# Routed attention and a gated FFN on one core: preparation placed by a table, one more pair turned on TensorE, v summed by adds, a last tile in parts

## The chip, the core and the metric

The kernel runs on one core of one Trainium2 chip. The time is the device time of the whole program in microseconds; for the kernel before it is the median of 3 runs. One further execution was profiled. Its instructions are named by engine: PE (TensorE), PEld (its weight loads), DVE (VectorE), ACT (ScalarE), POOL (GpSimd) and SP (SyncE, which here only issues DMAs).

## The reference

Attention in which a query sees only the keys of its own cluster, followed by a gated FFN. Shapes: q, k, v 4 x 8 x 768 x 64 (batch, heads, rows, width), 16 centroids a head, FFN 512 to 1536 to 512, all float32.

```python
q_assign = argmax(q_n @ c_n.T); k_assign = argmax(k_n @ c_n.T)     # rows normalised
mask = q_assign[..., :, None] == k_assign[..., None, :]
scores = where(mask, (q @ k.T) / 8, -1e9)
attn = softmax(scores)                                              # + 1e-9 in the sum
x = (attn @ v).transpose(0, 2, 1, 3).reshape(3072, 512)
out = (sigmoid(x @ w_gate) * (x @ w_val)) @ w_out
```

## The kernel before, in words

**Steps.** The eight heads of a batch are taken in four pairs. One *step* is 128 keys against 384 queries of one head: a score matmul on PE (`do_scores`, L434), an exponential on ACT (L439), and, two steps later, three matmuls with v (`do_av`, L451). A head has 12 steps, a batch 96, the program 384; the step number runs through all batches. In every batch the last pair (heads 6 and 7) is taken in two halves of queries, so its four runs have six steps each, and head 7 is first used at step 78 of the batch.

**Mask.** Nothing compares clusters. Each head has a tile T of 80 rows: 64 of turned k and q and 16 of one-hot planes, for k the one-hot and for q minus 1920 wherever the cluster is another one. The score matmul over 80 rows thus adds the mask. To build T: the float32 data is split into a high and a low half in fp16 (tile hl: a cast, then a subtraction), turned, matmul'd with the centroids (logits lg), the maximum is picked (tile oh), the one-hots are turned and evicted into rows 64 to 79.

**Two ways to do that.** `pieces` (batch 0) turns on PE: tu (PE transposes, L545), ev (eviction, L556 on DVE or L554 on ACT), lg (L248), pk (a maximum and two comparisons on DVE), ot (one-hots turned on PE, L582), pl0 and pl1 (their evictions, L592 and L596, or L594 on ACT); hi and lo are the split (L527, L534). `pair_prep` (batches 1 to 3) turns by DMA from SP's queue: sp (the split, L679 and L680), turn (a DMA transpose of hl into T), lgt (logits, L257, with a copy of their low half on ACT, L263), pk (five DVE instructions, L271 to L284), ot (a DMA transpose of the one-hots, L693) and hops (four small DMAs into T, L305).

**Sums of v.** Where a key is masked its exponential is 0, so a small multiple of the sum of all v is added before the division. In batch 0 PE sums (`v_sum_pe`, L200). In the others one DVE instruction reduces 6 rows of v a partition (`v_sum`, L182, strided), one matmul with ones adds the partitions (L188), and DVE scales (L193). When a head ends, DVE adds that sum to the result and takes reciprocals (`normalise`, L216 and L218), and POOL multiplies (L221); x is then turned by DMA, or for the last pair of batch 0 on PE (L470, evicted at L471).

**Order.** Every engine works through its instructions in the order in which the program issues them; the order is written by hand. `at(i, f)` puts f behind step i. The due times stand as offsets to the step in which a head is used: `OFF` for `pieces`, numbers in `pair_prep` for the others, constant for all heads. `OFF` counts 12 steps a head for head 7 too. The loads of the next inputs are issued 76 steps ahead, the weights one block every ten steps from step 8.

**FFN.** A batch's rows are computed in two halves of 384. `ffn_atoms` makes a list of small functions: 12 gate atoms (four matmuls into one PSUM bank, L319, a tanh on ACT, L325), 12 value atoms (L334, evicted with the product into hT on DVE, L339), and for each of three output tiles three atoms of four matmuls (L351), an eviction on ACT (L360) or DVE (L358) and a store (L361). `run_steps` puts the first half into a queue at step 92 of its batch and the second at step 8 of the next; `ffn_run` takes atoms out in every step, as long as a credit of 500 ns a step lasts (a gate or value atom is priced at 643 ns, an output atom at 864). What is left behind step 383 runs at the end. So PE has no FFN work in the first 92 steps.

**Buffers.** Scores, gates, values and logits share four PSUM banks (`ring`); output tiles and the turns on PE share two (`op`); av has two. Raw inputs have four buffers a kind.

**Lead-in.** Seven matmuls on a tile of zeros (`dummies`, L514) run while the first data is loaded; then the centroids are normalised and head 0 is prepared in two parts, and ACT loads the table for Exp (L158) before it evicts.

Of the kernel before, what the change touches and what calls it, by code (L numbers as in the profile page):

```python
# [16 lines left out]
def kernel(
# [152 lines left out]
    VA, SV = {}, {}  # L170

# [6 lines left out]
    def v_sum(b, p):  # L178
        s = svp.tile([128, 2, 65], HP, tag="vs", name="vs")
        POOL.memset(s[:, :, 64:65], float(NCH))  # L180
        with nc.allow_low_precision("sums of the fp16 values' sources"):
            DVE.tensor_reduce(  # L182
                s[:, :, 0:64], RAW["v", b, p].rearrange("p h c d -> p h d c"), AX.X, ALU.add
            )

        def rest():
            t = bank(130, name="vs_ps")
            PE.matmul(  # L188
                out=t, lhsT=ones, rhs=s.rearrange("p h d -> p (h d)"), start=True, stop=True
# [120 lines left out]
    def ffn_atoms(xT, t0, n, b, ch):  # L310
# [131 lines left out]
    def do_av(s):  # L442
# [13 lines left out]
        if last:  # L456
            normalise(av, nq, b, p, e, x[:, :, bass.ts(e, 64)])
            if e == 1:
                f = lambda: turn_x(b, p, x, 384 * s["h0"], nq, s["xT"])
                if b == 0 and p == NP - 1:  # L460
                    at(step_no[0] + 5, f)
                else:
                    f()

    def turn_x(b, p, x, o, nq, xT):
        dst = xT[:, p, o : o + 128 * nq].rearrange("p (c t) -> p c t", t=128)
        if b == 0 and p == NP - 1:
            ps = bank(NCH * 128, HP, name="x_ps")
# [11 lines left out]

    def run_bg(i):
# [3 lines left out]
    LA = 2  # L485
# [3 lines left out]
    def run_steps(heads, xT, second, first):  # L489

        done = 0
        for n, th in heads:
            for s in th():
                s["xT"] = xT
                do_scores(s)
                pend.append(s)
                if second and done == LAG:
                    second()
                if done == 84 + LAG:
                    first()  # L500
                ffn_run(FFN_NS)
                if len(pend) > LA:
                    do_av(pend.pop(0))
                run_bg(step_no[0])
                step_no[0] += 1
                done += 1

    LAG = 8
    FFN_NS = 500.0

    def dummies(n):
        for i in range(n):
            w = bank(512, name="wm")
            PE.matmul(out=w, lhsT=warm[:, 0:128], rhs=warm, start=True, stop=True)  # L514

    def pieces(p, e, parts=1):
# [7 lines left out]
        def hi(s, eng=None):  # L524
            if s == 0:
                st["hl"] = hlp.tile([128, 12, 128], HP, tag="hl", name="hl")
            (eng or DVE.tensor_copy)(  # L527
                st["hl"][:, 6 * s : 6 * s + 6, 0:64], RAW["kq"[s], 0, p][:, e]
            )

        def lo(s, eng=None, part=None):
# [3 lines left out]
                hl[:, :, 64:128], RAW["kq"[s], 0, p][:, e, a - 6 * s : z - 6 * s],  # L535
# [39 lines left out]
        def ot(part=0):  # L575
            n = NCH // parts
            st["oh", part] = []
            for r0_, m in ((64 * e, 64),) if parts == 1 else ((0, 32), (32, 32)):
                ps = turns(128 * n, name="oh_ps")
                st["oh", part].append(ps)  # L580
                for c in range(n):
                    PE.transpose(  # L582
                        ps[r0_ : r0_ + m, bass.ts(c, 128)],
                        ohx[p][:, n * part + c, r0_ : r0_ + m], identh,
                    )
# [33 lines left out]
    oh_zero(2)  # L619
    a["tu"](0, 0)  # L620
# [5 lines left out]
    a["ev"](1, None, 0)  # L626
# [142 lines left out]
```

## Time and profile before

| | us |
|---|---|
| median of 3 runs (lowest, highest) | 351.84 (350.81, 353.98) |
| the profiled execution's own time | 351.25 |
| its span, first to last instruction | 349.5 |
| busy in the span: PE, ACT, DVE, POOL | 331.3, 231.6, 181.4, 109.4 |
| first score matmul starts | 9.56 |
| end of the span behind the last PE matmul (345.44) | 4.0 |

In rows of the timeline the columns are: start, length, engine, line, operation, written tile <- read tiles, shape, count, and in brackets the idle time just before it with what ended it. Rows of groups give the busy time, the mean in ns and the idle time before them. A busy PE is a PE with a matmul in flight; consecutive matmuls overlap.

### The profile page before, as it was taken

Reading aid. Unit: us, or ns where it says so; the run is one execution under the profiler, and the core shown is the slowest. Engines: PE = TensorE matmul, PEld = TensorE weight load, DVE = VectorE, ACT = ScalarE, POOL = GpSimd, SP = SyncE. Lnnn points to the kernel's source line nnn. Section 1 sums busy time; section 2 is a strip of 40 time slices with the busy share of each in tenths; the row PEclk is TensorE's granted clock in tenths of the full one; section 3 lists DMA queues with packets and bytes.
Section 4 is the critical chain, followed back from the end, with each engine's and each line's share of the span. In section 5 each row is a group of like instructions: output and inputs, shape, how many; then the busy total and the mean of one; then the engine's idle time right before and its main releaser. Section 6 shows DMA issues by size and latency. Waiting matters only on the chain.

```text
span 349.5 us, 8661 instructions
## 1 busy us (share of the span) xinstructions
PE 331.3 (95%) x3272; PEld 204.6 (59%) x3272; DVE 181.4 (52%) x465; ACT 231.6 (66%) x531; POOL 109.4 (31%) x170
## 2 busy tenths in 40 slices
PE   7899987898999999999999999999999999999995
PEld 3766664565556655565656655566556655654652
DVE  4677876666536463657446563656354432441430
ACT  6478766776768876787768866787768766531330
POOL 5376966442313334333314233333301001100000
PEclk9699989899999999999999999999999999999999
DMA  7968999999357735767468536951542002101002
GB/s 231 375 122 125 205 240 203 201 215 255 76 115 218 129 135 126 201 147 185 92 118 233 134 103 144 226 104 33 122 119 48 10 3 86 52 0 62 30 0 90
DMA packets 83385, 46.40 MB, mean 133 GB/s; under 512 B 61584, under 2 KB 80272, under 8 KB 83344
## 3 DMA queue, kind: packets, MB, share of 16 engines
q1 hardware_dynamic: 77408, 41.11, 47.3%
q0 software_dynamic: 5792, 4.72, 9.6%
q8 instruction: 25, 0.41, 0.5%
q14 instruction: 16, 0.13, 0.1%
q10 hardware_dynamic: 144, 0.03, 0.0%
HBM read 28.34 MB, written 6.29 MB: 99 GB/s over the span
## 4 chain that ended last, share of the span: by engine, by line
PE 76%; DVE 9%; DMA 7%; issue 3%; ACT 2%; POOL 1%; POOLq 0%; ACTq 0%; DVEq 0%
PE o L351 17%; PE v L334 17%; PE g L319 15%; PE sc L434 13%; PE av L451 9%; DMA T<-hl 6%; PE lg L257 2%; DVE hT L339 2%; DVE vs L182 2%; ACT es L439 2%; PE t_ps L545 1%; DVE t L216 1%; DVE hl L679 1%; POOL hl L534 1%; PE lg L248 1%
## 5 line engine op out<-in xcount | busy, mean ns | idle before, releaser
L439 ACT ACTIVATE es<-sc 128x384 f16<-128x384 f32 x384 | 173.7, 492 | 60.7 <-PE sc L434 41.0
L434 PE MATMUL sc<-T 80*128 80x384 f16 x384 | 120.7, 334 | 2.5 <-DVE T L596 1.3
L451 PEld LDWEIGHTS <-es 128*128 128x128 f16 x1152 | 81.5, 99 | 57.1 <-ACT es L439 13.6
L451 PE MATMUL av<-va,es 128*128 128x65 f16 x1152 | 99.7, 196 | 2.5 <-DVE hl L679 0.6
L339 DVE SCALAR_TENSOR_TENSOR hT<-th,v 128x384 f16<-128x384 f32 x96 | 53.1, 553 | 76.6 <-PE av L451 46.2
L319 PE MATMUL g<-xTb,wg 128*128 128x384 f16 x384 | 78.6, 325 | 1.6 <-DVE xTb L471 0.4
L334 PE MATMUL v<-xTb,wv 128*128 128x384 f16 x384 | 78.1, 325 | 1.4 <-DVE hT L339 1.4
L351 PE MATMUL o<-wo,hT 128*128 128x512 f16 x288 | 71.3, 378 | 0.0
L325 ACT ACTIVATE th<-g 128x384 f32<-128x384 f32 x96 | 47.2, 492 | 28.6 <-DVE hT L339 16.3
L221 POOL TENSOR_TENSOR xp<-t,rec 128x384 f16<-128x384 f32 (+1 forms) x40 | 28.1, 702 | 118.5 <-DVE rec L218 54.7
L334 PEld LDWEIGHTS <-wv 128*128 128x128 f16 x384 | 37.2, 97 | 23.3 <-issue 3.5
L319 PEld LDWEIGHTS <-wg 128*128 128x128 f16 x384 | 37.2, 97 | 22.5 <-issue 2.2
L351 PEld LDWEIGHTS <-hT 128*128 128x128 f16 x288 | 28.0, 97 | 24.9
L434 PEld LDWEIGHTS <-T 80*128 80x128 f16 x384 | 37.6, 98 | 1.4 <-DVE T L592 0.5
L680 POOL TENSOR_TENSOR hl<-kraw,hl 128x384 f16<-128x384 f32 x24 | 21.9, 914 | 49.7 <-issue 38.8
L216 DVE TENSOR_TENSOR t<-av,sv 128x390 f32<-128x390 f32 (+1 forms) x40 | 19.1, 478 | 22.1 <-PE av L451 22.1
L680 POOL TENSOR_TENSOR hl<-qraw,hl 128x384 f16<-128x384 f32 x24 | 21.9, 912 | 11.0 <-DVE hl L679 10.9
L358 DVE TENSOR_SCALAR ob<-o 128x512 f32<-128x512 f32 x8 | 5.5, 692 | 33.1 <-PE o L351 33.1
L360 ACT ACTIVATE ob<-o 128x512 f32<-128x512 f32 x16 | 9.6, 597 | 17.1 <-PE o L351 17.0
L182 DVE TENSOR_REDUCE vs<-vraw 128x128 f16<-128x768 f32 x12 | 17.5, 1460 | 0.0
L257 PE MATMUL lg<-cm,T 128*128 128x32 f16 x288 | 11.0, 177 | 2.3 <-DMA T<-hl 2.3
L176 POOL CAST va<-vraw 128x768 f16<-128x768 f32 x15 | 13.1, 872 | 0.0
(70 smaller groups left out, 201.5 us busy)
## 6 DMA issues: line engine op xcount, KB each, us to landing
vraw<-in_v_dram SPq DMA_DIRECT2D x16, 384.0 KB, 5.1
out_dram<-ob SPq DMA_DIRECT2D x24, 256.0 KB, 2.2
kraw<-in_k_dram SPq DMA_DIRECT2D x15, 384.0 KB, 4.2
qraw<-in_q_dram SPq DMA_DIRECT2D x15, 384.0 KB, 4.5
wg<-in_moe_w_gate_dram POOLq DMA_DIRECT2D x4, 384.0 KB, 5.7
wv<-in_moe_w_val_dram POOLq DMA_DIRECT2D x4, 384.0 KB, 6.3
wo<-in_moe_w_out_dram POOLq DMA_DIRECT2D x2, 768.0 KB, 9.2
T<-ohT SPq DMA_DIRECT2D x48, 24.0 KB, 1.9
```

Source lines behind the costliest of these rows:

```text
L182: DVE.tensor_reduce(s[:, :, 0:64], RAW["v", b, p].rearrange("p h c d -> p h d c"), AX.X, ALU.add)
L216: DVE.tensor_tensor(t[:, 0:nq, :], av, sv, ALU.add)
L221: (eng or POOL).tensor_tensor(x, t[:, 0:nq, 0:64], bcast(rec[:, 0:nq], 64), ALU.mult)
L319: PE.matmul(out=g[:, 0:n], lhsT=wg[fc // WQ][:, dc, fc % WQ, :], rhs=xT[:, dc, t0 : t0 + n], start=(dc == 0), stop=(dc == NDC - 1),)
L325: ACT.activation(th[:, 0:n], g[:, 0:n], AF.Tanh, scale=0.5)
L334: PE.matmul(out=w[:, 0:n], lhsT=wv[fc // WQ][:, dc, fc % WQ, :], rhs=xT[:, dc, t0 : t0 + n], start=(dc == 0), stop=(dc == NDC - 1),)
L339: DVE.scalar_tensor_tensor(hT[:, fc, 0:n], st[0][:, 0:n], 1.0, w[:, 0:n], ALU.add, ALU.mult)
L351: PE.matmul(out=o, lhsT=hT[:, fc, bass.ts(t, 128)], rhs=wo[fc // 6][:, fc % 6, :], start=(fc == 0), stop=(fc == NFC - 1),)
L434: PE.matmul(out=sc.rearrange("p (c t) -> p c t", t=128), lhsT=s["k"], rhs=s["q"], start=True, stop=True,)
L439: ACT.activation(es, sc, AF.Exp, scale=SCALE)
L451: PE.matmul(out=av[:, s["c0"] + i, :], lhsT=s["es"][:, bass.ts(i, 128)], rhs=VA[b, p][:, e, s["j"], :], start=(first and i == 0), stop=(la ...
L680: POOL.tensor_tensor(hl[:, :, 64:128], r, hl[:, :, 0:64], ALU.subtract)
```

## The change

Every step number of the preparation, of the loads of weights and inputs, of the FFN's entries and its credit a step is now looked up in a table, `SCHED`. `h2ev1` is piece ev1 of head 2 in batch 0, `g0`, `g1` are heads 0 and 1 of batch 1; their numbers are steps of the program. `b1p2lg0` is a piece of pair 2 in batch 1, `b2...` of any pair in batches 2 and 3; their numbers are relative to the pair's first step. A name with E at its end puts a piece on another engine (A is ACT, D is DVE, P is POOL). `w..` and `wo.` are weights, `vc`, `vs`, `vu`, `vt` the parts of v's cast and sum, `lag` and `ns` the FFN's entry and credit, `dm` counts of spare matmuls.

- Batch 1's first pair is prepared by `pieces` and turned on PE (`npe: 1`), no longer by DMA.
- The first use of heads 6 and 7 is counted as it is (steps 72 and 78).
- The lead-in has 12 spare matmuls of 512 columns instead of 7, and 2, 6, 11 and 2 of 128 columns at four later places. ACT makes one more of the first evictions, loads the Exp table later, and gives a plane to DVE and the cast of v to POOL.
- `v_sum` adds with three DVE instructions in two pieces instead of one reduce.
- The last output tile of all is computed in column parts of 256, 128 and 128, each with its own eviction and store.

```diff
+SCHED = {
+    "halved0": 1, "npe": 1, "npe0": 4, "vs00": 5, "h1tu0": 0, "h1ev0": 0, "h1tu1": 0,
+    "h1ev1": 1, "h1lg": 2, "h1pk": 3, "h1ot": 6, "h1pl0": 10, "h1pl1": 11, "h2hi0": 0,
+    "h2lo0": 0, "h2hi1": 0, "h2lo1": 1, "h2tu0": 2, "h2ev0": 3, "h2tu1": 3, "h2ev1": 10,
+    "h2lg": 10, "h2pk": 12, "h2ot": 13, "h2pl0": 15, "h2pl1": 20, "h3hi0": 0, "h3lo0": 4,
+    "h3hi1": 1, "h3lo1": 4, "h3tu0": 11, "h3ev0": 12, "h3tu1": 15, "h3ev1": 16, "h3lg": 18,
+    "h3pk": 19, "h3ot": 20, "h3pl0": 24, "h3pl1": 30, "vc01": 13, "vs01": 24, "h4hi0": 4,
...
+    "h6lg": 63, "h6pk": 65, "h6ot": 67, "h6pl0": 69, "h6pl1": 69, "h7hi0": 22, "h7lo0": 40,
+    "h7hi1": 45, "h7lo1": 53, "h7tu0": 60, "h7ev0": 62, "h7tu1": 58, "h7ev1": 64, "h7lg": 65,
+    "h7pk": 65, "h7ot": 69, "h7pl0": 75, "h7pl1": 72, "vc03": 47, "vs03": 69, "g0hi0": 57,
+    "g0lo0": 66, "g0hi1": 67, "g0lo1": 70, "g0tu0": 77, "g0ev0": 78, "g0tu1": 81, "g0ev1": 81,
+    "g0lg": 81, "g0pk": 81, "g0ot": 87, "g0pl0": 87, "g0pl1": 92, "g1hi0": 69, "g1lo0": 78,
+    "g1hi1": 77, "g1lo1": 78, "g1tu0": 85, "g1ev0": 86, "g1tu1": 87, "g1ev1": 90, "g1lg": 93,
+    "g1pk": 93, "g1ot": 100, "g1pl0": 100, "g1pl1": 106, "w00": 3, "w01": 13, "w10": 26,
+    "w11": 20, "w20": 15, "w21": 35, "w30": 39, "w31": 65, "wo0": 73, "wo1": 91, "b1p0vc": -18,
+    "b1p0vs": -11, "b1p0vu": -2, "b1p0vt": 5, "b1p0ld": -80, "b1p1sp00": -59, "b1p1sp01": -53,
+    "b1p1tn0": -50, "b1p1lg0": -35, "b1p1pk0": -31, "b1p1sp10": -48, "b1p1sp11": -43,
+    "b1p1tn1": -40, "b1p1lg1": -24, "b1p1pk1": -24, "b1p1ot": -22, "b1p1hp0": -21,
...
+    "b1p2sp00": -58, "b1p2sp01": -54, "b1p2tn0": -54, "b1p2lg0": -32, "b1p2pk0": -29,
...
+    "b1p3vc": -15, "b1p3vs": -14, "b1p3vu": -5, "b1p3vt": 4, "b1p3ld": -79, "b2sp00": -59,
+    "b2sp01": -50, "b2tn0": -48, "b2lg0": -37, "b2pk0": -36, "b2sp10": -52, "b2sp11": -44,
+    "b2tn1": -40, "b2lg1": -27, "b2pk1": -27, "b2ot": -19, "b2hp0": -11, "b2hp1": -17,
+    "b2vc": -17, "b2vs": -15, "b2vu": -13, "b2vt": 4, "b2ld": -83, "xt30": 2, "xt31": 5,
+    "lag00": 8, "lag01": 7, "lag10": 6, "lag11": 10, "ns0": 530, "ns1": 470, "ns2": 500,
+    "ns3": 440, "dm0": 12, "dm1": 2, "dm2": 6, "dm3": 11, "dm4": 2, "la0": 2, "la1": 2,
+    "lgop": 0, "h2pl1E": "A", "h2lo0E": "D", "h4hi0E": "P", "h1ev0E": "A", "h3hi0E": "A",
+    "h4pl1E": "A", "g0hi1E": "A", "h5lo1E": "D", "h5ev0E": "A", "h6hi0E": "A", "g0ev1E": "A",
+    "h7hi1E": "P", "h4hi1E": "P", "h4lo0E": "D", "g1hi0E": "A", "h7hi0E": "A", "h3pl1E": "A",
+    "h4lo1E": "D", "h5lo0E": "D", "g1lo0E": "D", "h5hi1E": "A", "h3ev0E": "A", "h3hi1E": "A",
+    "h5hi0E": "P", "g0hi0E": "P",
+}
...
     def v_sum(b, p):
...
+        r, st = RAW["v", b, p], {}
+        def one():
+            st["a"] = vsp.tile([128, 2, 3, 64], FP, tag="va3", name="va3")
+            DVE.tensor_tensor(st["a"], r[:, :, 0:3], r[:, :, 3:6], ALU.add)
+        def two():
+            a = st["a"]
+            s = st["s"] = vss[(b * NP + p) % len(vss)]
+            t = vsp.tile([128, 2, 64], FP, tag="va1", name="va1")
+            DVE.tensor_tensor(t, a[:, :, 0], a[:, :, 1], ALU.add)
+            DVE.tensor_tensor(s[:, :, 0:64], t, a[:, :, 2], ALU.add)
...
+        def closing(t, a, z):
+            def f():
+                w = z - a
+                o = bank(w, name="o_end")
+                for fc in range(NFC):
+                    PE.matmul(
+                        out=o, lhsT=hT[:, fc, bass.ts(t, 128)],
+                        rhs=wo[fc // 6][:, fc % 6, a:z],
+                        start=(fc == 0), stop=(fc == NFC - 1),
+                    )
...
-    dummies(7)
+    dummies(SCHED.get("dm0", 7))
...
-    a["ev"](1, None, 0)
+    a["ev"](1, ACT, 0)
     centroid_d(cv)
     a["ev"](0, ACT, 1)
     a["ev"](1, ACT, 1)
-    v_cast(0, 0, ACT.copy)
+    ACT.activation(r1, warm[:, 0:1], AF.Exp)
     a["lg"](0)
     b_["hi"](0)
     b_["lo"](0)
+    v_cast(0, 0)
     a["lg"](1)
     a["pk"](0)
+    dummies(SCHED.get("dm2", 6), 128)
     a["ot"](0)
+    dummies(SCHED.get("dm3", 8), 128)
     a["pl"](0, None, 0)
-    a["pl"](1, ACT, 0)
+    a["pl"](1, None, 0)
...
+            lag = SCHED.get(f"lag{key}{i}", 8)
+            if b == B - 1 and i:
+                break
+            at(u + lag, lambda xT=xT, b=b, i=i: ffn_block(xT, 384 * i, 384, b, CH[i]))
...
+                ffn_run(SCHED.get(f"ns{b}", 500.0))
```

More of the change, by code (lines that the diff above doesn't have):

```diff
@@ L57 @@
     svp = pool("sv", 6)
+    vsp = pool("vs", 1)
     ohp = pool("oh", 2)
@@ L193, in rest @@
             DVE.tensor_scalar(sv.rearrange("p h d -> p (h d)"), t, TINY, None, ALU.mult)
-        return rest
+        return one, two, rest
     def v_sum_pe(b, p):
-        t = bank(130, name="vs_ps")
+        t = (turns if SCHED.get("lgop", 1) else bank)(130, FP, name="vs_ps")
         for j in range(NCH):
@@ L483, in run_bg, with dummies, pieces @@
             f()
-    LA = 2
+    LA = {0: SCHED.get("la0", 3), 1: SCHED.get("la1", 2)}
     pend = []
[L489 to L511, printed above, removed]
+    def dummies(n, m=512):
+        if not n:
+            return
+        w = bank(512, name="wm")
         for i in range(n):
-            w = bank(512, name="wm")
-            PE.matmul(out=w, lhsT=warm[:, 0:128], rhs=warm, start=True, stop=True)
-    def pieces(p, e, parts=1):
+            PE.matmul(out=w[:, 0:m], lhsT=warm[:, 0:128], rhs=warm[:, 0:m], start=True, stop=True)
+    def pieces(b, p, e, parts=1):
         h, st = 2 * p + e, {}
@@ L619 @@
     oh_zero(2)
+    for t in vss:
+        POOL.memset(t[:, :, 64:65], float(NCH))
+    dummies(SCHED.get("dm1", 3), 128)
     a["tu"](0, 0)
@@ L642, with halved, heads @@
     oh_zero(0)
+    def halved(b):
+        return SCHED.get("halved0", 1) if b == 0 else 1
+    def heads(b):
+        n = NP - halved(b)
+        out = [(p, e, [0, 1]) for p in range(n) for e in range(2)]
+        return out + [(p, e, [c]) for c in range(2) for p in range(n, NP) for e in range(2)]
+    USE, u = {}, 0
+    for p, e, c in heads(0):
+        USE.setdefault((p, e), u)
+        u += NCH * len(c)
+    at(0, lambda: dummies(SCHED.get("dm4", 2), 128))
     at(0, lambda: a["ot"](1))
@@ new lines @@
+    plan("vs00", 5, lambda: v_sum_pe(0, 0))
+    for b, p, e in P:
+        if b + p + e == 0:
+            continue
+        d = P[b, p, e]
+        u = USE[p, e] if b == 0 else 96 + 24 * p + 12 * e
+        for k_, o_ in OFF.items():
+            if b + p == 0:
+                if k_ not in first_b:
+                    continue
+                o_ = first_b[k_] - u
+            f = d[k_[:2]]
+            nm = f"{'hg'[b]}{2 * p + e}{k_}"
+            if k_[2:]:
+                eng = SCHED.get(nm + "E")
+                s_ = int(k_[2])
+                if k_[:2] == "hi":
+                    eng = eng and {"P": POOL.tensor_copy, "A": ACT.copy}[eng]
+                elif eng:
+                    eng = {"D": DVE, "A": ACT}[eng]
+                f = (lambda f=f, s_=s_, eng=eng: f(s_, eng)) if k_[:2] != "tu" else (
+                    lambda f=f, s_=s_: f(s_))
+            plan(nm, u + o_, f)
@@ L733 @@
+        for p, e, c in heads(b):
+            for s in head_steps(b, p, e, c):
+                s["xT"] = xT
+                do_scores(s)
+                pend.append(s)
+                ffn_run(SCHED.get(f"ns{b}", 500.0))
+                while len(pend) > LA[min(b, 1)]:
+                    do_av(pend.pop(0))
+                run_bg(step_no[0])
+                step_no[0] += 1
     while pend:
-        ffn_run(FFN_NS)
+        ffn_run(500.0)
         do_av(pend.pop(0))
+    assert not bg, sorted(bg)
```

151 lines of the change are left out of this document (78 added, 73 removed), and 11 rows, old and new, of the table SCHED.

## The prediction

> **What bounds the kernel now.** First the pace: each of the 384 steps issues one score matmul (tile sc), so the busy time by stretch, kept to that tile, counts steps. Columns: stretch, its length, PE busy (count), ACT busy (count), granted clock, DMA share, GB/s.
>
> ```profile
> 9.56:19.64 10.08, 4.72 (x13) 4.78 (x11) 0.66 1.01 357
> 19.64:44.73 25.09, 13.88 (x47) 19.89 (x48) 1.00 0.89 143
> 44.73:68.65 23.92, 12.22 (x36) 15.34 (x36) 0.86 1.08 205
> 71.37:148.98 77.61, 29.67 (x96) 44.16 (x97) 1.00 0.71 162
> 148.98:226.03 77.05, 29.65 (x97) 44.22 (x97) 1.00 0.65 151
> 226.03:300.90 74.87, 29.54 (x96) 43.74 (x97) 1.00 0.29 69
> ```
>
> The stretches are steps 0-11, 12-56, 57-92 (to the score of step 93), then batches 1, 2 and 3; counts hold what an edge cuts. Batch 0, which has no FFN beside it, has three paces: 0.84 us a step (10.08 / 12), 0.56 (25.09 / 45) and 0.66 (23.92 / 36). From step 93 on the FFN fills PE: 0.81, 0.80, and 0.78 in the last batch, beside which nothing is prepared. The same view for all engines (PE, PEld, DVE, ACT, POOL, clock, DMA):
>
> ```profile
> 6.54:9.96 3.42, 1.96 (x40) 1.29 (x37) 2.50 (x11) 2.29 (x6) 1.06 (x2) 1.00 1.02 342
> 9.96:16.78 6.82, 6.76 (x78) 5.40 (x75) 4.03 (x12) 2.90 (x6) 2.96 (x4) 0.50 1.07 379
> 19.64:44.73 25.09, 23.45 (x368) 16.19 (x367) 18.96 (x50) 19.89 (x48) 18.75 (x25) 1.00 0.89 143
> 57.75:61.16 3.41, 1.97 (x24) 1.11 (x25) 1.97 (x5) 2.12 (x6) 3.39 (x6) 1.00 1.08 210
> 61.16:64.57 3.41, 3.41 (x40) 2.49 (x39) 2.42 (x8) 3.35 (x9) 0.90 (x3) 0.50 0.78 115
> ```
>
> Twice a stretch with PE busy under 60% is followed by one at half clock. From 9.96 to 16.78 PE is full at half clock: the slow first steps are PE's. Next PE's own rows in order of time, in which two waits of batch 0 and 1 stand out: a mask plane evicted one step before its use, and a transpose by DMA that lands late.
>
> ```profile
> 59.30 0.32 PE L434 MATMUL sc<-T 80*128 80x384 f16 x1 [1.31 <-DVE T L596]
> ```
>
> ```profile
> 80.59 0.47 PE L257 MATMUL lg<-cm,T 128*128 128x32 f16 x12 [0.85 <-DMA T<-hl]
> ```
>
> Last, the FFN stretch: what DVE does, and PE beside it.
>
> ```profile
> 83.36 0.56 DVE L216 TENSOR_TENSOR t<-av,sv 128x390 f32<-128x390 f32 x1
> 83.95 0.19 DVE L218 RECIPROCAL rec<-t 128x6 f32<-128x6 f32 x1
> 84.06 1.46 DVE L182 TENSOR_REDUCE vs<-vraw 128x128 f16<-128x768 f32 x1
> 85.43 0.35 DVE L679 CAST hl<-kraw 128x384 f16<-128x384 f32 x1
> 85.70 0.55 DVE L339 SCALAR_TENSOR_TENSOR hT<-th,v 128x384 f16<-128x384 f32 x1
> ```
>
> ```profile
> 81.81 0.33 PE L434 MATMUL sc<-T 80*128 80x384 f16 x1
> 81.97 0.33 PE L334 MATMUL v<-xTb,wv 128*128 128x384 f16 x1
> ```
>
> ```profile
> 85.69 0.33 PE L434 MATMUL sc<-T 80*128 80x384 f16 x1
> 86.30 0.81 PE L334 MATMUL v<-xTb,wv 128*128 128x384 f16 x4 [0.28 <-DVE hT L339]
> ```
>
> The reduce of v stands right behind a normalisation (both fall at ten steps ahead of the pair's use), so hT begins only at 85.70 and its PSUM bank comes free late: the value matmul follows its score after 0.61 us, where 0.16 is usual (81.81 to 81.97). So PE sets the end everywhere, in batch 0 with waits on every engine. At the pace of its middle stretch, batch 0's 93 steps would take 52 us and not 59.1.
>
> **The change, part by part.** The sum is made against the profiled execution: 351.25 us, 1.75 over its span of 349.5. The median of the runs, 351.84, lies 0.6 above it.
>
> *Lead-in (first score at 9.56).*
>
> ```profile
> 1.32 3.17 PE L514 MATMUL wm<-warm 128*128 128x512 f16 x7 [1.32 <-POOL warm L79]
> 5.09 0.50 PE L545 MATMUL t_ps<-identh,hl 128*128 128x128 f16 x3 [0.60 <-DVE hl L534]
> ```
>
> ```profile
> 9.03 0.48 ACT L594 ACTIVATE T<-oh_ps 16x384 f16<-16x384 f16 x1
> ```
>
> Seven dummies last 3.17 us, the last of them 0.63 (3.17 less six intervals of 0.42). Twelve (dm0) end near 1.32 + 12 x 0.42 = 6.4, with dm1's two 6.5: PE's first turns come 1.4 us after 5.09. Won back: the second plane goes from ACT (ends 9.51, behind the cast of v) to DVE right behind the first (-0.3); one eviction leaves DVE for ACT, because the Exp table is loaded later (-0.36, estimated from 0.35 for casts of this size); the turns run at full clock (-0.35, half of two groups that take 0.35 each). Net +0.4; bounds -0.3 (the clock is granted early, dummies are half as long) and +1.4 (nothing is won back).
>
> *Steps 0-11 (10.08).* dm2, dm3 and dm4 put 19 small matmuls where PE is idle between 6.54 and 9.96 (1.46 of 3.42 us). If the clock then stays at 1.00, 6.8 us of full PE at half clock shrink to 3.4. Against it, ACT takes one eviction and two casts of h3 (0.83 + 2 x 0.49, rows below), DVE the subtraction of h2; and h1's planes come at steps 10 and 11 with an eviction of h2 between: three DVE instructions of 0.57 ahead of step 12, behind which PE waits some 0.6. Net -1.8; bounds 0 (clock as now) and -3.0.
>
> *Steps 12-56 (25.09).* Eight pieces go to ACT: h3ev0, h2pl1, h3pl1, h5ev0, h4pl1 (768 columns) and h7hi0, h6hi0, h5hi1 (384).
>
> ```profile
> L176 ACT CAST va<-vraw 128x768 f16<-128x768 f32 x1 | 0.8, 833 | 0.7 <-DMA vraw<-in_v_dram 0.7
> L527 ACT CAST hl<-qraw 128x384 f16<-128x384 f32 x1 | 0.5, 494 | 0.0
> ```
>
> No row has a 768-column eviction on ACT; the 768 cast is nearest: 5 x 0.83 + 3 x 0.49 = 5.6 us, where ACT has 25.09 - 19.89 = 5.2 idle. It becomes full; behind each such piece wait the next exponentials, their av and so PE. DVE loses these pieces but gains four subtractions; POOL is relieved. +1.5; bounds -0.5 (idle time covers it, shorter DVE bursts win) and +5.6 (all in the chain); nearer the cover, since most of ACT's idle time is there.
>
> *Steps 57-92 (23.92).* h7's planes go from steps 75 and 77 (its use is step 78, while the code counted 84) to 75 and 72: the 1.31 at 59.30 goes. Batch 1's first pair is turned by PE, and pair 1's logits come 15 and 16 steps behind their DMA turn instead of 11. The row of this stretch:
>
> ```profile
> L257 PE MATMUL lg<-cm,T 128*128 128x32 f16 x48 | 1.9, 180 | 1.5 <-DMA T<-hl 1.5
> ```
>
> 1.5 us of PE waiting for turned tiles. Added for two heads, from the chain of waits:
>
> ```profile
> 21.12 0.45 PE oh_ps L582 x6
> 22.31 0.57 DVE T L556
> 22.92 0.49 PE t_ps L545 x6
> 23.68 0.50 ACT es L439
> 24.87 0.58 PE lg L248 x24
> ```
>
> A head costs 2 x 0.49 + 0.58 + 0.45, less 0.48 (1.9 / 4) for the old logits: 1.5, the two 3.1 us of PE, partly after step 92. Their eight evictions are 0.57 each on DVE but one. The two turns, a turn of one-hots and four hops leave SP's queue and the DMA queues; what stands behind them there starts sooner. With the waits gone, this work lies in PE's latency gaps as it does in steps 12-56: 36 x 0.555 = 20.0. Net -4.0; bounds -1.0 (turns fill what the waits leave) and -5.0.
>
> *Step 106* (80.59): pair 2's turn moves to 22 steps ahead of its logits: -1.0 (0.85 and the ramp); bounds 0 and -1.1.
>
> *Sums of v.* Twelve reduces of 1.46 become adds over 384, 128 and 128 numbers. Nearest: t, 390 numbers, 0.56; for the others
>
> ```profile
> L193 DVE TENSOR_SCALAR sv<-vs_ps 128x130 f32<-128x130 f32 x12 | 3.5, 290 | 3.7 <-PE vs_ps L188 3.6
> ```
>
> 0.56 + 2 x 0.29 = 1.14, in two places (-15, -13), clear of the normalisation at -10. The hole at 86.30 is 0.45, the next one
>
> ```profile
> 87.35 0.33 PE L434 MATMUL sc<-T 80*128 80x384 f16 x1
> 87.82 0.49 PE L319 MATMUL g<-xTb,wg 128*128 128x384 f16 x2
> ```
>
> 0.31; of twelve sums six fall among gate and value atoms: 6 x 0.75 = 4.5. But a pick (five DVE instructions) now stands two steps ahead of that normalisation, so -2.5; bounds 0 and -4.6.
> The Trainium skill, page "SBUF — State Buffer", section "Who interferes with whom", says that a reduce on VectorE never contends with GpSimd, while an instruction with two SBUF inputs does and is blocked for the whole of the other. No row here shows such adds. By it an add may stand behind a POOL subtraction, this term be near 0 and the time 344.
>
> *Pacing.* One half of the FFN is credited with 24 x 643 + 9 x 864 ns = 23.2 us, so two at 500 a step last 92.8 of 96 steps: the queue runs dry before the next half, and PE waits for exponentials:
>
> ```profile
> 296.71 0.26 PE L451 MATMUL av<-va,es 128*128 128x65 f16 x3 [0.30 <-ACT es L439]
> ```
>
> With 470 in batch 1, 46.4 - 1.6 lasts to step 191, and the next half enters at 186; 440 in batch 3 stretches it further. Three such places, each 0.3 to 0.9 with the late steps around it: -2.0; bounds -0.5 and -2.6.
>
> *Tail.*
>
> ```profile
> 345.48 0.60 ACT L360 ACTIVATE ob<-o 128x512 f32<-128x512 f32 x1 [4.58 <-PE o L351]
> ```
>
> The last part has 128 columns: 0.29 (sv) instead of 0.60; 24 more matmuls cost PE about 0.1; the store, a quarter, is counted at -0.1. Net -0.3; bounds +0.3 and -0.8.
>
> Sum: 0.4 - 1.8 + 1.5 - 4.0 - 1.0 - 2.5 - 2.0 - 0.3 = -9.7. 349.5 - 9.7 + 1.75 = 341.55, said as **341.5 us**.
>
> **The rivals.**
> *The clock stays half in the first steps* (0.17). For it: 9.96 to 16.78 stayed half with PE 99% busy. Against: real matmuls fill the idle time ahead of it. Steps 0-11 win nothing: 341.5 + 1.8 = 343.3. The Trainium skill, "TensorE: Matmul & The Clock Gate", Part 4, says that transposes on PE do not count as busy for the clock; turns are among those matmuls, so the trace leaves it possible.
> *DVE is late all the same* (0.15): picks, adds and normalisations still meet, the holes stay: 341.5 + 2.5 = 344.
> *The DMA waits only move* (0.10): other logits meet unlanded turns, +2.5 in steps 57-92 and +1.0 at step 106: 345.
> *ACT becomes batch 0's bound* (0.08), the other side: its pieces, 1.8 + 5.6 and three of 1.8 in steps 57-92, all lie in the exponentials' chain. Steps 0-11 win nothing, 12-56 lose 5.6, 57-92 lose 1.8: 0.4 + 5.6 + 1.8 - 1.0 - 2.5 - 2.0 - 0.3 = +2.0, 353.2. It decides once steps 12-56 take 0.68 us each. For it: ACT is 79% busy there. Against: exponentials in a row are shorter than 0.49,
>
> ```profile
> 19.55 2.02 ACT L439 ACTIVATE es<-sc 128x384 f16<-128x384 f32 x5 [0.41 <-PE av L451]
> ```
>
> 0.40 each, so that ACT has more room than its busy time says.
>
> **How the numbers follow.** The forecast has 0.50. Of the others 0.42 lie at 343 to 345, two together at 346 to 348.5; terms nearer their good bounds reach 336.5. So 336.5 to 348, without the last rival. A measurement of this kernel tells about 1% from no change. Under 348.3 is faster: 0.87, the forecast and three rivals less a little for three of them together; within 1%: 0.09, that and most of the last rival; slower: 0.04, the rest of it.
>
> **What would show it.** Right: step 93's score near 64.8 (68.65 less 3.9); clock 1.00 from 10 us on; no logit matmul waiting over 0.3 for a DMA; no value or gate matmul over 0.4 behind its score in batches 1 to 3; the span's end 3.7 us or less behind PE's. Wrong: steps 12-56 over 30 us; half clock after 10 us; PE waiting for hT as at 86.30.

## The result, and the profile after

The changed kernel takes 343.12 us (median of 4 runs, 342.12 to 344.48) against 352.73 for the kernel before in 4 runs (350.81 to 353.98): a ratio of 0.9735, interval 0.9672 to 0.9798. The profiled execution took 342.54 us with a span of 340.8; the forecast was 341.5 with a span of 339.8.

The same view as in the prediction, busy time by stretch with the score tile alone, of the changed kernel: steps 0-11, 12-56, 57-92, then batches 1, 2 and, to its last score, 3. Columns: from and to, length, busy time and count on PE and on ACT, granted clock, DMA share, GB/s.

```profile
10.59:20.08 9.49, 3.55 (x13) 5.15 (x12) 1.00 1.09 364
20.08:44.45 24.37, 13.63 (x46) 18.46 (x45) 1.00 1.00 167
44.45:64.79 20.34, 10.77 (x38) 15.15 (x37) 1.00 0.89 161
68.11:142.87 74.76, 29.46 (x96) 43.83 (x96) 1.00 0.72 156
142.87:218.98 76.11, 29.54 (x96) 44.04 (x96) 1.00 0.67 154
218.98:287.70 68.72, 28.87 (x96) 43.20 (x95) 1.00 0.36 78
```

One correction: in the kernel before, the score of step 57 starts at 43.75; 44.73, where the prediction drew its line, is step 58. With the line at step 57 its two stretches, in the same columns, are

```profile
19.64:43.75 24.11, 13.56 (x47) 18.91 (x46) 1.00 0.87 139
43.75:68.65 24.90, 12.54 (x37) 16.32 (x38) 0.86 1.09 206
```

So the 8.7 us of span come from: first score +1.03 (9.56 to 10.59), steps 0-11 -0.59, 12-56 +0.26, 57-92 -4.56, from there to step 96 +0.60 (2.72 to 3.32), and from step 96 to the end -5.4. The last needs the batches and the tail together, because the new pacing leaves more FFN for the tail; all engines (length, then busy time and count of PE, PEld, DVE, ACT and POOL, the granted clock, the DMA share and GB/s), kernel before, then changed:

```profile
71.37:349.50 278.13, 269.62 (x2456) 162.40 (x2454) 132.46 (x328) 182.45 (x419) 66.54 (x103) 1.00 0.48 112
```

```profile
68.11:340.80 272.69, 268.92 (x2503) 165.19 (x2501) 134.37 (x360) 182.44 (x420) 66.03 (x91) 1.00 0.50 114
```

PE is idle for 3.8 us of it where it was 8.5, with 47 matmuls more. Of the waits of PE that the profile lists there, 3.6 us before, 0.2 is left; the longest row before, for hT (us in all, times, longest), has no counterpart:

```profile
PE v L334 <- DVE hT L339: 1.4, 5, 0.3
```

The granted clock of this execution is a 9 in all 40 slices of the page's second part. What is left of waits in the busy end of batch 0, PE, then DVE, then POOL:

```profile
58.40 0.46 PE L299 MATMUL lg<-cm,T 128*128 128x16 f16 x12 [0.61 <-ACT T L615]
...
61.09 0.45 PE L308 MATMUL lg<-cm,T 128*128 128x32 f16 x12 [0.43 <-DVE oh L631]
```

```profile
56.91 2.94 DVE L595 TENSOR_TENSOR hl<-kraw,hl 128x384 f16<-128x384 f32 x1
```

```profile
56.84 0.93 POOL L774 TENSOR_TENSOR hl<-qraw,hl 128x384 f16<-128x384 f32 x1
57.72 0.91 POOL L595 TENSOR_TENSOR hl<-qraw,hl 128x384 f16<-128x384 f32 x1
58.57 0.15 POOL L220 MEMSET va<- 128x12 f16 x1
58.62 0.82 POOL L221 CAST va<-vraw 128x768 f16<-128x768 f32 x1
```

A subtraction that the table gave to DVE (g1lo0) takes 2.94 us and ends 0.4 us behind three POOL instructions with inputs in SBUF. And the adds, by groups:

```profile
L228 DVE TENSOR_TENSOR va<-vraw 128x384 f32<-128x384 f32 x12 | 6.9, 571 | 0.0
...
L235 DVE TENSOR_TENSOR vs<-va,va 128x128 f16<-128x128 f32 x12 | 5.7, 471 | 0.4
...
L234 DVE TENSOR_TENSOR va<-va 128x128 f32<-128x128 f32 x12 | 5.0, 416 | 0.2
```

0.571 + 0.471 + 0.416 = 1.458 us a sum: as much as the reduce's 1.460. DVE is busy for 181.5 us, before 181.4. Nothing was saved there; only the place and the length of a piece changed.

### The profile page after: what moved, and what is told of

Read it like the earlier page. It is cut to its first block, busy times and chain, and to the rows that moved or that the text cites. A ratio compares the mean times of both kernels' runs of the same rounds, so it can differ in the third digit from the quotient of the medians.

```text
span 340.8 us, 8867 instructions
## 1 busy us (share of the span) xinstructions
PE 330.0 (97%) x3382; PEld 206.7 (61%) x3382; DVE 181.5 (53%) x482; ACT 236.3 (69%) x542; POOL 107.8 (32%) x162
## 4 chain that ended last, share of the span: by engine, by line
PE 89%; DVE 5%; ACT 3%; issue 1%; DMA 1%; POOL 0%; DVEq 0%; ACTq 0%; POOLq 0%
PE v L385 19%; PE g L370 18%; PE o L402 17%; PE sc L512 16%; PE av L529 10%; PE lg L308 2%; PE wm L575 2%; ACT es L517 2%; PE t_ps L606 1%; DVE hl L595 1%; PE oh_ps L643 1%; DMA xTb<-xp 1%; PE o_end L426 1%; PE lg L299 1%; DVE T L617 1%
## 5 line engine op out<-in xcount | busy, mean ns | idle before, releaser
L512 PE MATMUL sc<-T 80*128 80x384 f16 x384 | 117.1, 327 | 0.5 <-DVE T L657 0.2
L529 PEld LDWEIGHTS <-es 128*128 128x128 f16 x1152 | 79.7, 98 | 52.5 <-ACT es L517 11.8
L529 PE MATMUL av<-va,es 128*128 128x65 f16 x1152 | 98.1, 194 | 2.4 <-ACT es L517 1.5
L402 PE MATMUL o<-wo,hT 128*128 128x512 f16 x276 | 68.6, 378 | 0.0
L402 PEld LDWEIGHTS <-hT 128*128 128x128 f16 x276 | 26.7, 97 | 23.3
L774 POOL TENSOR_TENSOR hl<-qraw,hl 128x384 f16<-128x384 f32 x22 | 20.6, 937 | 32.9 <-DVE hl L773 32.8
L774 POOL TENSOR_TENSOR hl<-kraw,hl 128x384 f16<-128x384 f32 x22 | 20.1, 919 | 12.3 <-issue 8.9
L322 DVE TENSOR_TENSOR lgs<-lg,lglo 128x192 f32<-128x192 f32 x22 | 7.8, 355 | 19.7 <-ACT lglo L314 19.2
L221 POOL CAST va<-vraw 128x768 f16<-128x768 f32 x16 | 14.2, 888 | 0.0
L606 PE MATMUL t_ps<-identh,hl 128*128 128x128 f16 x120 | 10.2, 221 | 0.4 <-DVE T L653 0.4
```

What stands on the lines that cost most here:

```text
L221: (cast or POOL.tensor_copy)(va[:, :, :, 0:64], RAW["v", b, p])
L402: PE.matmul(out=o, lhsT=hT[:, fc, bass.ts(t, 128)], rhs=wo[fc // 6][:, fc % 6, :], start=(fc == 0), stop=(fc == NFC - 1),)
L512: PE.matmul(out=sc.rearrange("p (c t) -> p c t", t=128), lhsT=s["k"], rhs=s["q"], start=True, stop=True,)
L529: PE.matmul(out=av[:, s["c0"] + i, :], lhsT=s["es"][:, bass.ts(i, 128)], rhs=VA[b, p][:, e, s["j"], :], start=(first and i == 0), stop=(la ...
L774: POOL.tensor_tensor(hl[:, :, 64:128], r, hl[:, :, 0:64], ALU.subtract)
```

## The experiments

Times are medians. Each ratio, with its interval, is to runs of the kernel before on the same chip (351.13 to 351.86 us). The changed kernel has 0.9735. Stretches are cut at the same steps as above. A difference in us is one of medians, to the 343.12 of the changed kernel, whose four runs were taken apart from these; by the ratios the differences come out 0.3 to 1.5 us higher, so one below about 1.5 us is not told from none. What a stretch took is from the one profiled execution of each kernel. A `...` marks what is left out of a diff.

**Without the spare matmuls**

```diff
-    "ns3": 440, "dm0": 12, "dm1": 2, "dm2": 6, "dm3": 11, "dm4": 2, "la0": 2, "la1": 2,
+    "ns3": 440, "dm0": 7, "dm1": 0, "dm2": 0, "dm3": 0, "dm4": 0, "la0": 2, "la1": 2,
```

> The changed kernel with 7 wide dummies and none of the small ones (as before the change), all else changed. Theory (the spare matmuls hold the clock): the first turns start near 5.1 us and the first score near 9.6, 1.0 earlier than in the changed kernel (10.59), but the granted clock falls to 0.50 within the first 17 us again and steps 0-11 take 11 us or more instead of 9.49; in all +0.5 to +2 us on the changed kernel. Rival (the clock follows how full PE is kept by the work itself, and the denser table is enough): clock 1.00 throughout, steps 0-11 as in the changed kernel, first score 1 us earlier, in all -1 us.

343.09 us, 0.9777 (0.9717 to 0.9836). First score at 8.62, steps 0-11:

```profile
8.62:19.13 10.51, 4.46 (x12) 5.14 (x12) 0.70 1.08 361
```

The clock fell as the theory said, and the steps cost 1.0 us more; but the first score came 2 us earlier in this execution. The spare matmuls keep the clock and win nothing that these runs can tell: 0.0 us by the medians, 1.5 by the ratios.

**Spare matmuls only behind the first logits**

```diff
-    "ns3": 440, "dm0": 12, "dm1": 2, "dm2": 6, "dm3": 11, "dm4": 2, "la0": 2, "la1": 2,
+    "ns3": 440, "dm0": 7, "dm1": 0, "dm2": 6, "dm3": 11, "dm4": 2, "la0": 2, "la1": 2,
```

> The changed kernel with 7 wide dummies instead of 12 and none ahead of the first turns, but the 19 small ones that stand behind the first logits kept. Theory (the wide ones delay the first turns, the small ones alone keep the clock): first score near 9.0 to 9.3 us, clock 1.00 after it, steps 0-11 9.5 us: -0.5 to -1.2 us on the changed kernel. Rival (the clock needs the wide ones): half clock within the first 17 us and steps 0-11 at 10.5 us: within 0.5 us of the changed kernel.

343.53 us, 0.9758 (0.9730 to 0.9785). First score at 8.89, and

```profile
8.89:18.39 9.50, 3.55 (x12) 5.14 (x12) 1.00 1.07 370
42.77:64.47 21.70, 11.40 (x38) 15.22 (x37) 0.92 0.91 164
```

In the first steps the theory holds in both parts: the small ones alone keep the clock, and the wide ones cost the lead-in. Not in the whole: steps 57-92 had 3.41 us, 59.60 to 63.01, at half clock and took 1.4 us longer than in the changed kernel.

**The reduce at the place of the first add**

```diff
-            st["a"] = vsp.tile([128, 2, 3, 64], FP, tag="va3", name="va3")
-            DVE.tensor_tensor(st["a"], r[:, :, 0:3], r[:, :, 3:6], ALU.add)
+            s = st["s"] = vss[(b * NP + p) % len(vss)]
+            with nc.allow_low_precision("sums of the fp16 values' sources"):
+                DVE.tensor_reduce(
+                    s[:, :, 0:64], r.rearrange("p h c d -> p h d c"), AX.X, ALU.add
+                )
...
+            return
```

> The changed kernel with v summed by the one strided reduce again, at the place in the table where the first add stands (the second piece is empty). Theory (placement wins, not the kind of instruction: the three adds measured 0.571 + 0.416 + 0.471 = 1.458 us, the reduce 1.46): within 0.5 us of the changed kernel; batches 1 and 2 (steps 96 to 287) within 0.5 us of 150.9. Rival (one long instruction delays hT wherever it stands): each of some nine sums costs 0.3 to 0.75 us again, +2.5 to +4.5 us in all.

345.14 us, 0.9823 (0.9778 to 0.9867), 2.0 above the changed kernel: between the two theories. In its profile batch 2 is no longer (75.65, changed 76.11), batch 1 is by 2.05, and steps 57-92 by 1.96, where a stretch of half clock lies. So the place is not all of it. That the reduce costs time only where it does not stand free is a reading of these stretches; the half clock is in them too.

**The adds at the old offsets**

```diff
-    "b2vc": -17, "b2vs": -15, "b2vu": -13, "b2vt": 4, "b2ld": -83, "xt30": 2, "xt31": 5,
+    "b2vc": -17, "b2vs": -10, "b2vu": -8, "b2vt": -6, "b2ld": -83, "xt30": 2, "xt31": 5,
```

and the same for the pairs of batch 1.

> The changed kernel with the adds at the offsets of before (first at use-10, second at -8, matmul at -6, behind the normalisation at -10). Theory (placement wins): the holes come back in part, the first add (0.57) behind the normalisation (0.56 + 0.19): +1 to +3 us in batches 1 and 2. Rival (splitting wins): the adds leave room between them for hT, within 0.5 us of the changed kernel.

346.59 us, 0.9872 (0.9821 to 0.9922), 3.5 above. Its worst place, DVE, then PE:

```profile
234.20 0.74 DVE L228 TENSOR_TENSOR va<-vraw 128x384 f32<-128x384 f32 x1
234.98 0.89 DVE L234 TENSOR_TENSOR va<-va 128x128 f32<-128x128 f32 x1
235.90 0.30 DVE L235 TENSOR_TENSOR vs<-va,va 128x128 f16<-128x128 f32 x1
```

```profile
236.25 0.23 PE L239 MATMUL vs_ps<-vs,ones 128*128 128x130 f16 x1 [0.72 <-DVE vs L235]
```

An add of 128 numbers lasts 0.89 us, three times its own 0.30, and the matmul with ones, two steps behind, makes PE wait. POOL runs two instructions there, 233.70 to 235.72. Batches 1 and 2 take 3.7 us more, a little over the theory's 3: place wins. The place of the matmul with ones (4 steps behind use in batches 2 and 3 of the table) was moved back too and is part of it: PE's waits for that matmul come to 1.4 us.

**The reduce moved in the kernel before**

```diff
-        at(use - 10, lambda: st.update(f=v_sum(b, p)))
+        at(use - 15, lambda: st.update(f=v_sum(b, p)))
```

> The kernel before with its reduce of v moved from ten steps ahead of the pair's use to fifteen, nothing else. Theory (the reduce cost time only because it stood behind a normalisation): the waits of value matmuls for hT (0.28 at 86.30 and its like) go, -1.5 to -4 us. Rival (1.46 us on DVE delays hT anywhere): within 1 us of the kernel before.

351.36 us, 0.998 (0.9947 to 1.0014): no change. The value matmul at the place of the 86.30 wait now follows its score at once, but the gate matmul two steps later is as late as before, and PE waits longer for turned tiles:

```profile
87.00 0.81 PE L334 MATMUL v<-xTb,wv 128*128 128x384 f16 x4
...
88.06 0.33 PE L434 MATMUL sc<-T 80*128 80x384 f16 x1
88.53 0.65 PE L319 MATMUL g<-xTb,wg 128*128 128x384 f16 x3
```

```profile
81.73 0.44 PE L257 MATMUL lg<-cm,T 128*128 128x32 f16 x11 [1.98 <-DMA T<-hl]
```

The waits for hT that the profile lists (1.4 us behind step 96 before) are gone, as the theory said, but those for turned tiles and for x rose from 1.3 to 4.6 us. So what the reduce's place won did not reach the end. (The profiled execution, 353.56, is one of the longer ones.)

**The old pacing**

```diff
-    "lag00": 8, "lag01": 7, "lag10": 6, "lag11": 10, "ns0": 530, "ns1": 470, "ns2": 500,
-    "ns3": 440, "dm0": 12, "dm1": 2, "dm2": 6, "dm3": 11, "dm4": 2, "la0": 2, "la1": 2,
+    "lag00": 7, "lag01": 7, "lag10": 7, "lag11": 7, "ns0": 500, "ns1": 500, "ns2": 500,
+    "ns3": 500, "dm0": 12, "dm1": 2, "dm2": 6, "dm3": 11, "dm4": 2, "la0": 2, "la1": 2,
```

> The changed kernel with 500 ns of credit in every step and the FFN halves entering at the steps of before. Theory (pacing closes three holes where the queue runs dry, 0.5 to 1.2 us each in the kernel before): PE waits near steps 186, 282 and 378 again, +1.5 to +2.5 us. Rival (these holes were the lateness of x and not an empty queue): within 0.5 us.

347.6 us, 0.9893 (0.9833 to 0.9953), 4.5 above, more than the theory's 2.5. From step 96 to the end it takes 278.0 us (changed 272.7). PE waits where the queue is dry, at steps 186, 282 and 378 (0.30 each), and then for x:

```profile
142.05 0.26 PE L529 MATMUL av<-va,es 128*128 128x65 f16 x3 [0.30 <-ACT es L517]
```

```profile
220.81 0.40 PE L370 MATMUL g<-xTb,wg 128*128 128x384 f16 x1 [1.79 <-DMA xTb<-xp]
```

So the rival, late x, holds in part: 2.1 us of waits for x, where the changed kernel's profile lists none. The long one leaves PE busy for 1.41 of the 3.42 us up to 220.92, and the next 3.41 us have half clock; in steps 57-92, too, 3.41 us have it (22.22 us, changed 20.34). At a mean clock of 1.00 two of its runs took 346.0 and 346.4, two of the changed kernel's 342.1 and 342.5.

**The new pacing in the kernel before**

```diff
-                if second and done == LAG:
+                if second and done == (8 if heads_b == 1 else 11):
...
-                if done == 84 + LAG:
+                if done == (93 if heads_b == 0 else 91):
...
-                ffn_run(FFN_NS)
+                ffn_run((530.0, 470.0, 500.0, 440.0)[heads_b])
```

`heads_b` is the batch; the FFN's entries are thus those of the changed kernel.

> The kernel before with the new pacing alone: 530, 470, 500 and 440 ns of credit, FFN halves entering as in the changed kernel. Theory (the pacing by itself closes the dry-queue holes): PE no longer waits near steps 186 and 282, -1 to -2.5 us on the kernel before. Rival (it pays only with the table that was laid beside it; undoing it there cost 4.5 us): within 1 us of the kernel before.

347.26 us, 0.9869 (0.9834 to 0.9904): -4.5 us by itself, more than the theory's 2.5. From step 96 to the end:

```profile
72.22:346.20 273.98, 267.92 (x2460) 162.95 (x2458) 134.45 (x326) 182.58 (x420) 66.86 (x103) 1.00 0.50 112
```

274.0 us, of the kernel before 278.1, of the changed one 272.7. Done and undone, pacing has the same size. Of the two parts that were tried alone it is the one that won. The three waits on a dry queue are gone, 0.9 us; where the rest comes from is not shown, since the waits for hT (1.5 us, before 1.4) and for x (0.6, before 0.4) stayed. Nor was the credit tried apart from the entries.

**Batch 1's first pair by DMA again**

```diff
-    "halved0": 1, "npe": 1, "npe0": 4, "vs00": 5, "h1tu0": 0, "h1ev0": 0, "h1tu1": 0,
+    "halved0": 1, "npe": 0, "npe0": 4, "vs00": 5, "h1tu0": 0, "h1ev0": 0, "h1tu1": 0,
```

> The changed kernel with batch 1's first pair prepared through DMA transposes again, at the offsets of before. Theory (a turn by DMA makes PE wait in the busy end of batch 0, and the PE work of the other way lies in gaps): a logit matmul waits for its turn, steps 57-92 take 21 to 23 us instead of 20.3, in all +1 to +3 us. Rival (PE is the bound and the turns cost it 3.1 us): steps 57 to 96 get shorter, -1 to -2 us in all.

348.35 us, 0.9914 (0.9881 to 0.9948), 5.2 above, more than the theory's 3; the profiled execution, 345.95, is the shortest of the four. Steps 12-56 take 26.37 us (24.37), with waits for DVE at steps 48, 49 and 54 (0.75, 0.41, 0.60), and 57-92 20.98 (20.34), 6.4 us of them at half clock. The logits wait for a DMA turn for 0.35 us only. The wait at step 78 is back, for a plane that has three steps of notice:

```profile
55.62 0.42 DVE L328 TENSOR_TENSOR oh<-lgs,mx 128x96 f16<-128x96 f32 x2
56.08 0.19 DVE L335 TENSOR_SCALAR oh<-oh 128x96 f16<-128x96 f16 x1
56.30 0.56 DVE L657 TENSOR_SCALAR T<-oh_ps 16x768 f16<-16x768 f16 x1
56.89 0.36 DVE L773 CAST hl<-kraw 128x384 f16<-128x384 f32 x1
...
58.10 0.56 DVE L653 COPY T<-oh_ps 16x768 f16<-16x768 f16 x1
```

```profile
58.72 0.34 PE L512 MATMUL sc<-T 80*128 80x384 f16 x1 [1.19 <-DVE T L653]
```

DVE comes to the plane at 58.10, behind the pick and the casts that the other way of preparing asks of it at this point. So the cost came through DVE more than through the DMA that the theory named.

**Head 7's plane late again**

```diff
-    "h7pk": 65, "h7ot": 69, "h7pl0": 75, "h7pl1": 72, "vc03": 47, "vs03": 69, "g0hi0": 57,
+    "h7pk": 65, "h7ot": 69, "h7pl0": 75, "h7pl1": 77, "vc03": 47, "vs03": 69, "g0hi0": 57,
```

> The changed kernel with one number changed: the second plane of head 7 at step 77, one ahead of its use, as before, instead of 72. Theory (the 59.30 wait came from the due time alone): a score matmul waits 0.5 to 1.5 us for that plane near step 78, steps 57-92 +0.5 to +1.5 us, more where the clock then halves. Rival (the wait came from DVE's backlog, which the table has taken away): under 0.3 us.

342.63 us, 0.9737 (0.9705 to 0.9769): nothing lost. PE at step 78:

```profile
54.30 0.34 PE L512 MATMUL sc<-T 80*128 80x384 f16 x1
```

No wait for DVE: the plane is done at 54.25. The theory falls and the rival holds. In the kernel before DVE had worked without a pause from 53.89 on:

```profile
57.82 0.84 DVE L679 CAST hl<-qraw 128x384 f16<-128x384 f32 x1
58.69 0.56 DVE L596 TENSOR_SCALAR T<-oh_ps 16x768 f16<-16x768 f16 x1
```

The pick and the turn of head 7's one-hots stayed five steps earlier than before (65 and 69 instead of 70 and 74), so the run clears the due time of this plane alone.

**ACT's pieces back on DVE**

```diff
-    "lgop": 0, "h2pl1E": "A", "h2lo0E": "D", "h4hi0E": "P", "h1ev0E": "A", "h3hi0E": "A",
...
+    "lgop": 0,  "h2lo0E": "D", "h4hi0E": "P",  
```

and the other eleven in the same way.

> The changed kernel with its fourteen pieces on ACT back on DVE. Rival (the prediction's own step: ACT pieces stand in the exponentials' chain and cost 1.5 us in steps 12-56): steps 12-56 take 23.5 us or less instead of 24.37. Theory (they lie in ACT's idle time, and DVE is the one that would be late): steps 0-92 together take +1 to +4 us, most of it in steps 0-11, where DVE has the most to do.

348.65 us, 0.9901 (0.9861 to 0.9940), 5.5 above. Steps 0-11 9.96 (9.49), and

```profile
20.58:45.31 24.73, 13.96 (x45) 18.71 (x45) 0.93 0.98 162
45.31:70.58 25.27, 11.89 (x38) 15.60 (x37) 0.86 0.90 175
```

Steps 12-56 are no shorter in all, but the comparison is not even: the run was ahead of the changed kernel from step 16 on, by 1.1 us at step 30, until a stretch of half clock, 34.54 to 37.95. The changed kernel has waits of PE for exponentials in steps 12-56 that this run has not:

```profile
PE av L529 <- ACT es L517: 1.5, 5, 0.4
```

So the rival is not refuted. Steps 57-92 lose 4.9, and not steps 0-11 the most, as the theory had it: 1.2 up to head 7's plane at step 78, which comes 0.83 late, 2.5 at step 82, because the eviction of g0 now stands on DVE behind the blocked subtraction, and the rest behind it, where 6.83 us have half clock:

```profile
62.89 0.49 PE L299 MATMUL lg<-cm,T 128*128 128x16 f16 x12 [3.04 <-DVE T L617]
```

**That subtraction on POOL**

```diff
-    "h4lo1E": "D", "h5lo0E": "D", "g1lo0E": "D", "h5hi1E": "A", "h3ev0E": "A", "h3hi1E": "A",
+    "h4lo1E": "D", "h5lo0E": "D",  "h5hi1E": "A", "h3ev0E": "A", "h3hi1E": "A",
```

> The changed kernel with one subtraction (g1lo0, step 78) on POOL instead of DVE. In the changed kernel it held DVE for 2.94 us beside three POOL instructions in a row, where the same one takes 0.55. Theory (DVE was locked out by POOL, and PE's waits near steps 81 and 85 follow from it): no DVE subtraction over 1 us, steps 57-92 19.3 to 19.9 us, no half clock near 60 us, -0.3 to -1.5 us. Rival (PE's wait there is for ACT's eviction, and POOL gets another 0.9 us of work): within 0.3 us, or slower.

342.55 us, 0.9758 (0.9726 to 0.9790), not to be told from the changed kernel. DVE's subtractions of k:

```profile
L595 DVE TENSOR_TENSOR hl<-kraw,hl 128x384 f16<-128x384 f32 x3 | 1.8, 606 | 0.1
```

The blocking is gone (0.61 on average), steps 57-92 take 19.83 us (20.34) at full clock, PE's wait near step 85 is gone, the one at step 81 for ACT is not: half of the theory.

**The three together**: the subtraction on POOL, spare matmuls only behind the first logits, and g0's logits and pick a step and two after the eviction.

```diff
-    "g0lg": 81, "g0pk": 81, "g0ot": 87, "g0pl0": 87, "g0pl1": 92, "g1hi0": 69, "g1lo0": 78,
+    "g0lg": 82, "g0pk": 83, "g0ot": 87, "g0pl0": 87, "g0pl1": 92, "g1hi0": 69, "g1lo0": 78,
...
```

> The changed kernel with that subtraction on POOL, 7 wide dummies and none ahead of the first turns, and the logits and pick of batch 1's head 0 at steps 82 and 83 instead of both at 81, in the step of their last eviction. Theory: first score near 9.0 (-1.0 us or more on average over the clock's phase), steps 57-92 at 19 to 20 us without half clock: 341 us or less, -1 to -2.5 us on the changed kernel. Rival (the lead-in's gain is lost in the waits of batch 0, as it was with the 7 dummies alone): within 0.7 us of the changed kernel.

341.22 us, 0.9720 (0.9685 to 0.9756): 1.9 below the changed kernel's median, 0.5 by the ratios, so not clear of it by the intervals. First score at 8.87, steps 0-11 9.49, and steps 57-92

```profile
42.73:62.30 19.57, 10.78 (x38) 15.27 (x37) 1.00 0.89 165
```

## Why the prediction was right

The total was 1.0 us of span short of the forecast's 9.7. By halves, cut at step 93, batch 0 was forecast at -3.9 and gave -3.9 (+1.03 - 0.59 + 0.26 - 4.56), the rest at -5.8 and gave -4.8 (+0.60 - 5.4). The direction and the places of the gains were right; the close fit is partly luck: in batch 0 one term missed by +1.2 and another by -1.2, and behind it pacing was worth twice its term and made up for others that are smaller than theirs. Of the signs, step 93's score came at 64.79 (64.8 was said), no logits waited over 0.3 us for a DMA, and three gate or value matmuls stand over 0.4 behind their score (0.46 to 0.54) where none was to, eleven in the kernel before.

- *Lead-in* (+0.4, profile +1.03). The direction was right, and the size depends on when the full clock comes. Two executions with the same lead-in, the changed kernel and the one with the adds at the old offsets:

```profile
1.32 5.52 PE L575 MATMUL wm<-warm 128*128 128x512 f16 x14 [1.32 <-POOL warm L124]
```

```profile
1.32 4.32 PE L575 MATMUL wm<-warm 128*128 128x512 f16 x14 [1.32 <-POOL warm L124]
```

The same fourteen dummies take 5.52 or 4.32 us, and the first score comes at 10.59 or 9.18. The Trainium skill, "TensorE: Matmul & The Clock Gate", Part 1, says that the window in which the clock is judged runs freely of the kernel's start; these two rows agree, 1.2 us apart. Wide dummies start 0.43 us apart until 4.28 us in the second execution and 0.22 apart behind it; in the first all are 0.43 apart. Eight executions have this lead-in: their first scores come at 9.18 to 10.62, later the longer the dummies take, 9.84 on average. Three with the lead-in of before have 9.56, 8.75 and 9.39. On the averages the term is +0.6.
- *Steps 0-11* (-1.8, measured -0.59). The clock is kept, as forecast, but a full clock is worth only 1.0 us there (10.51 without spare matmuls against 9.49), because part of the time is not PE's: it waits 1.1 us for DVE there at full clock (0.70 and 0.39). What was too large is the halving of 6.8 us to 3.4. The rival of a half clock did not come true; what it cites of the Trainium skill ("TensorE: Matmul & The Clock Gate", Part 4), that turns on PE do not count as busy, stays open, since no run here held turns alone.
- *Steps 12-56* (+1.5, measured +0.26; with the line at step 58, where the prediction drew it, -0.16). The cost is there: PE waits 1.5 us for exponentials in five places, where the kernel before and the run without ACT's pieces have no such row. What made up for it was not measured apart, and what the pieces cost in all stays open, since the run without them fell to half clock in this stretch.
- *Steps 57-92* (-4.0, measured -4.56; -4.14 with the prediction's line; -3.96 with the stretch behind it, as FFN atoms enter a step later). The size was right. The step that failed is the 1.31 us of head 7's plane, put down to its due time: moved back to 77, it cost nothing. DVE's backlog made the wait, and the change of batch 1's pair from DMA to PE and ACT's help took it away: without the one or the other a wait for that head's planes is back at step 78, 1.19 or 0.83 us.
- *Step 106*: no logit matmul waits for a DMA there any more, as forecast.
- *Sums of v* (-2.5). The price of an add was wrong: 128 numbers were taken as 0.29 and took 0.42 and 0.47 on average, so that nothing is saved on DVE. The sentence that the prediction takes from the Trainium skill ("SBUF — State Buffer", "Who interferes with whom") was right in kind: adds of 0.30 became 0.89 beside POOL, a subtraction of 0.55 became 2.94. In the changed kernel the place counts: 3.5 us when the places are undone, about 2 when the three are one. In the kernel before the place alone won nothing, so the size of the term stays open.
- *Pacing* (-2.0). Mis-sized: 4.5 us, both ways. Of seven executions with the same table behind step 96, the changed kernel's own is the shortest (272.7 from there to the end; the six others, runs above, 273.3 to 274.2), and pacing alone took the kernel before to 274.0, with 43 matmuls fewer there. So little of the -3.8 that step 106, the sums and the tail were to bring together is seen on top of it.
- *Tail* (-0.3). Mis-sized: the last matmul ends 3.06 us ahead of the span's end, before 4.02. The last eviction takes 0.29, as taken, but the store was counted at -0.1 and gave about -0.7: from the end of the last eviction to the end of the span 2.7 us pass, before 3.4.

```profile
337.74 0.29 DVE L433 TENSOR_SCALAR ob_end<-o_end 128x128 f32<-128x128 f32 x1 [0.38 <-PE o_end L426]
```

The single undoings add up to more than the whole (3.5 + 4.5 + 5.2 + 5.5): they are not independent, and several of the runs also have half clock for 3 to 7 us near 60 us, which the changed kernel's profile has not. What decides on that, the traces show in part. The granted clock holds for stretches of 3.41 us. From step 57 to step 86 the changed kernel and the run with spare matmuls only behind the first logits agree step by step within 0.02 us. In that run nearly all of the waits at steps 81 and 85 falls into one stretch, 56.18 to 59.60, PE is busy for 2.33 of its 3.42 us, and the next one is at half clock. In the changed kernel the two waits fall into two stretches, with PE busy for 2.72 and 2.82, and the clock stays full. So the same waits cost or do not cost half clock by where the stretches lie; with the wait at step 85 taken away, neither of two traces has it. How often the changed kernel falls into it is open.

## What to carry to other kernels

Where one engine is full in the long stretch, look first at whether its queue of filler work runs dry at a seam: 6 to 12% less credit a step in two batches, with the entries moved by a few steps, was worth 4.5 us of 352 here, and adds in place of a reduce saved DVE nothing. Price an instruction at the place where it will stand, with what runs beside it: the same add cost 0.30 or 0.89 us. And to learn what a part of a change is worth, do it alone and undo it alone: of the two parts that were run both ways, pacing gave the same figure, the place of the sums 3.5 us and nothing.

## What the runs showed of the hardware

A VectorE subtraction with two SBUF inputs lasted as long as three GpSimd instructions in a row beside it, 2.94 us instead of 0.55, in the changed kernel and again without ACT's pieces; with that one moved to GpSimd, VectorE's subtractions of k took 0.61 on average. Exponentials of 0.49 us on ScalarE overlap, four in 1.64 us, so that ScalarE takes on more than its busy time says. The moment at which the full clock is granted moved the first score by 1.4 us between executions with the same lead-in. Waits of 0.6 and 0.4 us on TensorE were followed by half clock when one stretch of 3.41 us held nearly all of both, and not when they fell into two.
